# A kernel of attention and a two-layer network: the order of each engine's instructions written out, and other engines for some copies, scalings and relus

## The chip, the cores and the metric

The kernel runs on one core of a Trainium2 chip. A core has five engines with queues of their own: TensorE (PE, matmuls), VectorE (DVE), ScalarE (ACT), GpSimd (POOL) and SyncE (SP, which here only issues transfers). Each engine does its instructions in the order in which the program lists them; an instruction that waits holds up everything behind it on its engine. The time is that of one execution on the device in microseconds (us), and the median of several runs is given.

## The reference

Two parts stand one behind the other; all is float32.

```
scores = q @ k^T / 8                        # B=4, H=8, S=576, D=64; causal mask
a      = softmax(scores)
local  = a @ v
q_p    = where(q > 0, q, exp(q) - 1) + 1
mem    = (q_p @ M_prev) / (q_p . z_prev + 1e-6)
g      = 1 / (1 + exp(-beta))               # one per head
x      = g * mem + (1 - g) * local          # -> 2304 tokens x 512
r      = max(x @ w_in, 0)                   # 512 x 2048
out    = (s * r*r + b) @ w_out              # 2048 x 512
```

## The kernel before

**Attention.** The 32 heads are handled as 16 pairs (`attention(g)`, g = 0 to 15; four pairs make a batch). A pair goes through these steps. PE makes the scores (L383) in three visits, each over some of five row tiles `i`; DVE adds the mask and takes the row minimum of the negated scores (L390, `red`); ACT takes the exponential and its row sum (L396, `ex`); DVE makes the reciprocal of the sums (L435, L436); DVE or POOL scales the probabilities (L402, `scale`, by the table `SCAL`). Beside it `phi(g)` makes q_p from q: a relu (L319, L321 or L323 on ACT, DVE or POOL by `RELU`), an exponential on ACT (L324), a combination on DVE (L325), a product with z (L329, by `ZMUL`), a row sum on DVE (L331) and two products with its reciprocal (L342, by `PUTS`), which go into gaps of the probabilities' tile P. So one transposed tile holds both kinds of weights. PE transposes P in four banks (L463), 58 transposes for a pair; ACT or DVE copies each bank in two halves out of PSUM (L472 to L479, `copy`, by `COPY`); then PE makes the pair's output product (L514) from them, with M_prev and v in the tile V. ACT and DVE split the result into two parts of float32r (L535 and L536, tiles xs and x4).

**Network, first layer.** x @ w_in is made from those split parts, with three matmuls for one product (L580 to L582). 41 of these products, each in two halves of six matmuls, are placed among the attention (`first`), where PE has nothing else; ACT's relu (L603) and a transfer of SP to the DRAM tile r_d follow. They need the split results of the four pairs of a batch, and w_in, which is converted in 20 pieces by ACT, DVE and POOL (`convert`, L560 to L573; `HIGH` and `LOW` say on which engine its two parts are made). The rest of the first layer and the second layer follow behind the attention.

**What sets the order.** All steps of the attention are recorded in a `Plan` (`add`), each with its engine, a duration, a rank, what it reads and writes, and the PSUM tiles it takes (pool S: two tiles of 1024 columns, pool T: four of 512). `deal` then plays them through: at each point each engine takes, among the steps that could start, the one with the lowest rank, and for PE some rules on the changes between its three modes (`full`, `row`, `col`) come first. What it picks is the order in which the instructions are issued. Where PE would be idle in that play, `waits` puts in matmuls whose result is not used (L272, "filling" matmuls). The stages behind the attention are written in another way, by `later` and `tick`, and the change does not touch them.

Of the kernel before, what the change touches and what calls it, by code (L numbers as in the profile page):

```python
# [43 lines left out]
class Plan:  # L44
# [8 lines left out]
    TURN = 110  # L53
    HOLD, WORK, WAIT = (2.5, 3), (1, 5), (0.05, 0.05)
# [23 lines left out]
    def deal(self):  # L78
        ready = {}
# [4 lines left out]

        def put(s):
            s["at"] = max([0.0] + [
                d["end"] + (0.0 if d["eng"] == s["eng"] == "PE" else self.LAT + s["slack"]) for d in s["deps"]])
            ready.setdefault(s["eng"], []).append(s)

        for s in self.steps:  # L90
            if not s["need"]:
                put(s)
        while any(ready.values()):
            best = None
            for eng, some in ready.items():
                t0 = clock.get(eng, 0.0)
                able = []
                for s in some:
                    t = max(t0, s["at"], port if s["port"] else 0.0)
                    for place, pool in s["take"]:  # L100
                        if place is not None:
                            free = sorted(x for x in self.free[pool] if x is not None)
                            n = sum(1 for q in s["take"] if q[1] == pool)
                            t = max(t, free[n - 1] + s["slack"]) if len(free) >= n else None
                            break
                    if t is not None:
                        able.append((t, s))
                if not able:
                    continue
                first = min(t for t, _ in able)  # L110
                now = [(t, s) for t, s in able if t <= first + 0.02]
                if eng == "PE":
                    late = t0 >= self.TURN
                    wait = 0.15 if mode == "full" else self.WAIT[late]
                    same = [(t, s) for t, s in able if s["mode"] == mode and t <= max(t0 + wait, first + 0.02)]
                    rest = [(t, s) for t, s in now if s["mode"] != "full"]
                    if mode == "full" and rest and (
                            max(first - s["at"] for _, s in rest) >= self.HOLD[late] or sum(s["cost"] for _, s in rest) >= self.WORK[late]):
                        now = rest
                    elif same:  # L120
                        now = same
                    elif rest:
                        now = rest
                t, s = min(now, key=lambda x: (x[1]["rank"], x[1]["n"]))
                if best is None or t < best[0]:
# [46 lines left out]
def attention_moe_kernel(  # L172
# [469 lines left out]
    for g in range(NPAIR):  # L642
# [6 lines left out]
        if g % NP == NP - 1:  # L649
# [303 lines left out]
```

## Time and profile before

| | us |
|---|---|
| runs shown: median (lowest to highest, 3 runs) | 552.17 (550.9 to 552.63) |
| profiled execution: first to last instruction (its span) | 549.2 |
| PE busy | 537.4 (98%) |
| ACT busy | 397.7 (72%) |
| DVE busy | 396.5 (72%) |
| POOL busy | 259.6 (47%) |

The span is from the first to the last instruction of the profiled execution; the page gives no other time of that execution. The median of the runs is 3.0 us above the span. Busy time of PE holds the filling matmuls and matmuls that wait while they are in the pipeline, so it isn't a measure of work. A line number is the line of the instruction in the kernel before. In the views below an instruction reads as line, operation, the tile that it writes, `<-`, the tiles that it reads.

### The profile page before, as it was taken

To read this page: it belongs to the slowest core of one execution; us is meant where nothing else is said; L and a number is where in the kernel's file an instruction comes from. 1 tells how busy PE (TensorE), PEld (TensorE's weight loads), DVE (VectorE), ACT (ScalarE), POOL (GpSimd) and SP (SyncE) were. 2 spreads that over 40 slices of the span, in tenths; PEclk is the share of its full clock that TensorE was granted. 3 is DMA by queue.
4 is the path that set the end of the run, shared out by engine and by line. 5 is a ranking of instruction groups with operands and counts; after the bars stand their busy time and mean duration, and the time that the engine had idled before them with its cause. 6 is when DMAs were issued, how large, how long until landed. Compare 5 with 4: busy or idle time off the path is not lost.

```text
span 549.2 us, 11418 instructions
## 1 busy us (share of the span) xinstructions
PE 537.4 (98%) x4078; PEld 443.5 (81%) x4078; DVE 396.5 (72%) x979; ACT 397.7 (72%) x875; POOL 259.6 (47%) x273
## 2 busy tenths in 40 slices
PE   8998999999999999999999999999999999999997
PEld 6666777777777777777778888889999999999996
DVE  5999999999896643234239897434797897888772
ACT  6987898867678945466346577859987987887840
POOL 5882464441445751433100000507669668768760
PEclk9999899999999999999999999999999999999999
DMA  5556676754445333321166655448335344353101
GB/s 187 193 154 187 223 232 174 233 151 156 126 111 175 113 123 106 109 83 57 59 249 258 234 209 187 148 142 291 106 111 167 107 143 137 110 173 103 39 30 38
DMA packets 56665, 81.50 MB, mean 148 GB/s; under 512 B 7584, under 2 KB 39072, under 8 KB 56608
## 3 DMA queue, kind: packets, MB, share of 16 engines
q1 hardware_dynamic: 54064, 78.63, 44.3%
q10 hardware_dynamic: 2544, 2.14, 1.2%
q8 instruction: 32, 0.52, 0.4%
q14 instruction: 25, 0.20, 0.1%
HBM read 57.15 MB, written 23.59 MB: 147 GB/s over the span
## 4 chain that ended last, share of the span: by engine, by line
PE 85%; DVE 8%; ACT 2%; POOL 1%; DMA 1%; issue 1%; DVEq 0%; ACTq 0%; POOLq 0%
PE yps L808 12%; PE yps L812 11%; PE sb L514 7%; PE sb L383 6%; PE hps L580 5%; PE hps L581 5%; PE hps L582 5%; PE yps L811 5%; PE yps L810 5%; PE tb L463 4%; PE tb L580 4%; PE tb L581 3%; PE tb L582 3%; DVE P L390 3%; PE sb L580 3%; PE sb L581 2%
## 5 line engine op out<-in xcount | busy, mean ns | idle before, releaser
L402 POOL TENSOR_SCALAR P<-P,sr,omg 128x192 f32<-128x192 f32 (+4 forms) x118 | 75.9, 657 | 66.2 <-DVE sr L436 41.4
L396 ACT ACTIVATE P<-P,mn 128x448 f32<-128x448 f32 (+4 forms) x160 | 88.5, 559 | 22.0 <-DVE mn L390 20.8
L812 PE MATMUL yps<-rb,op 128*128 128x256 f32 x360 | 101.1, 281 | 0.0
L390 DVE CUSTOM_DVE_ANT_0 P<-sb,mask 128x448 f32<-128x448 f32 (+4 forms) x160 | 71.1, 483 | 17.7 <-PE sb L383 17.6
L808 PE MATMUL yps<-rb,op 128*128 128x512 f32 x216 | 76.9, 397 | 0.0
L812 PEld LDWEIGHTS yps<-rb,op 128*128 128x128 f32 x360 | 67.9, 189 | 0.0
L383 PE MATMUL sb<-qk 64*128 64x288 f32 (+4 forms) x384 | 57.8, 411 | 1.7 <-DMA qk<-in_qk_t_dram 0.9
L788 POOL TENSOR_TENSOR sum<-src 128x512 f32<-128x512 f32 x10 | 12.9, 1294 | 90.6 <-ACT src L772 75.9
L796 POOL TENSOR_TENSOR op<-src,op 128x512 fp32r<-128x512 f32 x30 | 44.0, 1490 | 20.1 <-ACT op L795 20.1
L819 DVE TENSOR_TENSOR yu<-yu,yps 128x256 f32<-128x256 f32 x90 | 36.5, 414 | 21.5 <-PE yps L812 20.4
L383 PEld LDWEIGHTS sb<-qk 64*128 64x128 f32 x384 | 35.6, 187 | 16.2 <-issue 6.1
L463 PEld LDWEIGHTS tb<-ident,P 64*128 64x128 f32 x928 | 37.3, 141 | 13.6 <-issue 3.5
L808 PEld LDWEIGHTS yps<-rb,op 128*128 128x128 f32 x216 | 40.6, 188 | 9.0
L463 PE MATMUL tb<-ident,P 64*128 64x64 f32 x928 | 42.3, 228 | 4.4 <-DVE P L402 2.4
L810 PE MATMUL yps<-rb,op 128*128 128x256 f32 x144 | 40.5, 281 | 0.0
L811 PE MATMUL yps<-rb,op 128*128 128x256 f32 x144 | 40.5, 281 | 0.0
L795 ACT CAST op<-src 128x512 fp32r<-128x512 f32 x50 | 30.4, 614 | 11.9 <-PE yps L812 7.5
L796 DVE TENSOR_TENSOR op<-sum,op 128x512 fp32r<-128x512 f32 x36 | 37.7, 1048 | 0.3 <-ACT op L795 0.2
L472 ACT COPY pt<-tb 128x512 f32<-128x512 f32 x54 | 29.0, 586 | 12.2 <-PE tb L463 7.8
L587 ACT ACTIVATE r<-hps 128x256 f32<-128x256 f32 x62 | 21.8, 384 | 18.5 <-DMA r_d<-r 14.5
L796 POOL TENSOR_TENSOR op<-w1H,op 128x512 fp32r<-128x512 f32 x24 | 34.9, 1482 | 0.0
L396 ACT ACTIVATION_READ_ACCUMULATOR P<-P,mn 128x1 f32 x160 | 31.0, 194 | 0.0
(171 smaller groups left out, 1548.2 us busy)
## 6 DMA issues: line engine op xcount, KB each, us to landing
r_d<-r SPq DMA_DIRECT2D x41, 256.0 KB, 2.4
src<-r_d SPq DMA_DIRECT2D x20, 512.0 KB, 4.8
qk<-in_qk_t_dram SPq DMA_DIRECT2D x15, 576.0 KB, 4.2
raw<-in_moe_w_out_dram SPq DMA_DIRECT2D x16, 512.0 KB, 5.8
w1H<-r_d SPq DMA_DIRECT2D x16, 512.0 KB, 4.4
xa<-in_moe_w_in_dram SPq DMA_DIRECT2D x12, 512.0 KB, 4.5
r_d<-r SPq DMA_DIRECT2D x48, 128.0 KB, 2.0
qs<-in_q_rows_dram SPq DMA_DIRECT2D x16, 320.0 KB, 3.8
```

The source lines that it names most:

```text
L383: nc.tensor.matmul(at(ps, j, o, n), lhsT=qk[rs, 128 * i:128 * i + 128], rhs=qk[rs, S + 64 + c0:S + 64 + c0 + n], start=True, stop=True, ti ...
L390: nc.vector.tensor_tensor_reduce(P[:, j, PB[i] + 64:PB[i] + 64 + n], at(ps, j, o, n), m, -SCALE, 3.0e38, ALU.add, ALU.min, mn[:, j, i:i + 1])
L396: nc.scalar.activation(pt, pt, AF.Exp, scale=-1.0, bias=mn[:, j, i:i + 1], accum_out=sm[:, j, i, 0:1])
L402: e.tensor_scalar(pt, pt, sr[:, j, i:i + 1], omg[:, h:h + 1], ALU.mult, ALU.mult)
L463: nc.tensor.transpose(TB[ps[h]][:, o[h]:o[h] + 64], P[rs, j, c:c + 128], ident[rs, rs], tile_position=(64 * h, 0))
L580: nc.tensor.matmul(ps, lhsT=wH[:, p, fs], rhs=xs[:, 0], start=p == 0, stop=False)
L581: nc.tensor.matmul(ps, lhsT=wH[:, p, fs], rhs=xs[:, 1], start=False, stop=False)
L796: (nc.gpsimd if m in ONPOOL else nc.vector).tensor_sub(L, x, H.bitcast(F32))
L808: nc.tensor.matmul(tile, lhsT=H, rhs=B, start=f == 0, stop=False)
L810: nc.tensor.matmul(ps, lhsT=H, rhs=B[:, 0], start=f == 0, stop=False)
L811: nc.tensor.matmul(ps, lhsT=H, rhs=B[:, 1], start=False, stop=False)
L812: nc.tensor.matmul(ps, lhsT=L, rhs=B[:, 0], start=False, stop=f == KF - 1)
```

## The change

`deal` takes a list `ORDER` with one number for each of the 1402 steps of the attention: on each engine the steps are issued by rising number, and nothing is picked any more. The rules for picking and their constants go. A step's start is still worked out in the play, for the order between the engines and for the filling matmuls, with durations that are partly new. The tables `RELU`, `ZMUL`, `PUTS`, `COPY`, `SCAL`, `HIGH`, `LOW` and `HOME` (the PSUM pool of an FFN product) have new letters: A is ACT, D is DVE, P is POOL. Of the 160 scalings 56 are on DVE, before 42; of the 32 products of phi with its norm 16, before 6; of the 16 products with z 3, before 6. The work on PE is the same, except that 26 filling matmuls are issued, before 35.

```diff
-    def deal(self):
-        ready = {}
+    def deal(self, order):
+        rows = {}
+        for s in sorted(self.steps, key=lambda s: order[s["n"]]):
+            rows.setdefault(s["eng"], []).append(s)
+        for row in rows.values():
+            row.reverse()
...
+            for eng, row in rows.items():
+                if not row or row[-1]["need"]:
                     continue
...
+                s = row[-1]
+                t = max([clock.get(eng, 0.0), port if s["port"] else 0.0] + [
+                    d["end"] + (0.0 if d["eng"] == eng == "PE" else self.LAT) for d in s["deps"]])
...
-    RELU = "AAPAADPAADAAAAAA"
-    ZMUL = "PPPDDDDDDPPPPPPP"
-    PUTS = "PPPDPPPPDDPPPPPP"
-    COPY = ["ADAD", "DAAD", "AAAD", "AAAA", "AAAA", "AAAA", "AAAA", "AAAD", "DDAD", "DAAD", ] + ["AAAD"] * 6
-    SCAL = ["PPPPP", "PPPPP", "DPPPP", "DDDDD", "DPPPP", "PPPDD", "PPPDD", "DDDDD", "PPPDD", "PPDDD", ] + ["PPPPP"] * 6
-    HIGH, LOW = "AAPAPAAAPPAAPPAAPAPA", "DPPDDPDPDDPDDDDDDPDP"
+    RELU = "AAAAAAAADAAADDDP"
+    ZMUL = "PDPDDPPPPPPPPPPP"
+    PUTS = "DDPDPPDDPPPPDDPD"
+    COPY = ["AAAD", "AAAA", "AAAA", "AAAA", "AAAA", "AAAA", "DAAA", "AADD", "AADA", "AAAA", "AAAA", "AADD", "DADA", "DADA", "ADAA", "DDDD"]
+    SCAL = ["PPPPP", "PDPPP", "DPPPP", "PPPPP", "PPPPP", "PDDPD", "PPDPD", "PPPPD", "DDDPP", "DDDPP", "PPPDP", "DDPPD", "PPPDP", "PDPPD", "PDPDP", "DDDDD"]
+    HIGH, LOW = "PPPAAAPAPAAAAAAAAAAA", "PDPDDPPPDDPDDDPPPDDP"
...
-    SCD = (0.11, 0.18, 0.26, 0.34, 0.42)
+    SCD = (0.22, 0.29, 0.36, 0.42, 0.49)
...
-    HOME = "TTTTTTTTTSTTTTTTTTTTTSTSSSTTSSSTSTTSSSTSS"
+    HOME = "TTTTTTTTTTSTTTSTTTTTTTSSSTTTTTSTTTTTSTSSS"
...
+    ORDER = [
+        0, 3, 5, 363, 13, 15, 21, 32, 1, 4, 7, 2, 6, 8, 30, 33, 36, 40, 50, 59, 80, 87, 84, 12, 19, 25, 16, 18, 17, 22, 23, 28, 39, 55, 61, 86, 70, 57, 20,
...
-        for step in plan.deal():
+        for step in plan.deal(ORDER):
```

The rows below are the instructions as the built program lists them on an engine; the line numbers of the changed kernel are lower by 30 in this part (L402 is L372 there). First DVE, before, with the last scalings of pair 3 (P_124 is the tile P of pairs 1, 3, 5, P_123 that of pairs 0, 2, 4; xs are split results of pair 2):

```order
L536 TENSOR_TENSOR xs<-tb_99,xs 128x256
L571 TENSOR_TENSOR w0L<-w_106,w0H 128x256
L564 SCALAR_TENSOR_TENSOR w_107<-xa_105,w_107 128x256
L402 TENSOR_SCALAR P_124<-P_124,sr_122,omg 128x192
L402 TENSOR_SCALAR P_124<-P_124,sr_122,omg 128x320 x2
L390 ISA P_123,mn_117<-sb_97,mask 128x448
L390 ISA mn_117 128x1
L402 TENSOR_SCALAR P_124<-P_124,sr_122,omg 128x64 x2
L402 TENSOR_SCALAR P_124<-P_124,sr_122,omg 128x576 x2
```

DVE in the changed kernel, from the last reciprocal of pair 3 to the last instruction that its output product needs:

```order
L406 RECIPROCAL sr_122<-sr_122 128x2
L312 TENSOR_TENSOR P_124<-qs_114,nrm_116 128x3x2x64
L360 ISA P_123,mn_117<-sb_97,mask 128x576
L360 ISA mn_117 128x1
L506 TENSOR_TENSOR x_141<-tb_100,x_141 128x64
L506 TENSOR_TENSOR xs<-tb_100,xs 128x256
L506 TENSOR_TENSOR xs<-tb_99,xs 128x256
L531 TENSOR_SCALAR w_106<-w_106 128x256
L360 ISA P_123,mn_117<-sb_96,mask 128x576
L360 ISA mn_117 128x1
L532 SCALAR_TENSOR_TENSOR w_106<-xa_103,w_106 128x256
L312 TENSOR_TENSOR P_124<-qs_114,nrm_116 128x2x2x64
```

The scalings of pair 3 are no longer on DVE; reductions of the next pair stand there, and the products of phi with its norm come last.

PE before, from the last score visit ahead of pair 3's output product (L514) on:

```order
L383 MATMUL sb_96<-qk_109 128x288
L514 MATMUL tb_99<-F_128,V_126 64x320 x2
L514 MATMUL tb_99<-pt,V_126 64x256 x2
L514 MATMUL tb_99<-F_128,V_126 64x128 x2
L514 MATMUL tb_101<-F_128,V_126 64x256 x2
L514 MATMUL tb_101<-pt,V_126 64x256 x6
L514 MATMUL tb_101<-F_128,V_126 64x128 x2
L383 MATMUL sb_97<-qk_110 128x448 x2
L383 MATMUL sb_97<-qk_110 128x64 x2
L383 MATMUL sb_96<-qk_110 128x320 x2
L383 MATMUL sb_96<-qk_110 128x192 x2
L580 MATMUL tb_98<-xs,w0H 128x512
```

PE in the changed kernel at the same product (L484 there):

```order
L353 MATMUL sb_96<-qk_110 128x320 x2
L353 MATMUL sb_96<-qk_110 128x192 x2
L484 MATMUL tb_98<-F_128,V_126 64x320 x2
L484 MATMUL tb_98<-pt,V_126 64x256 x2
L484 MATMUL tb_98<-F_128,V_126 64x128 x2
L484 MATMUL tb_99<-F_128,V_126 64x256 x2
L484 MATMUL tb_99<-pt,V_126 64x256 x6
L484 MATMUL tb_99<-F_128,V_126 64x128 x2
L550 MATMUL tb_100<-xs,w0H 128x512
```

The first two score visits of pair 5 (`qk_110`) are now ahead of the product, the second of them right before it, and the first layer's matmuls begin right behind it.

ACT before, at the copies of pair 1's transposes (L472 to L479; tiles F and pt are the copies):

```order
L472 COPY pt<-tb_98 128x8x64
L472 COPY pt<-tb_100 128x8x64
L324 ACTIVATE qs_113<-qs_113 128x640
L396 ACTIVATE P_123,sm_119<-P_123,mn_117 128x576
L474 COPY F_128<-tb_98 128x2x4x64
L474 COPY F_128<-tb_100 128x2x4x64
L396 ACTIVATE P_123,sm_119<-P_123,mn_117 128x576
```

ACT in the changed kernel at the same copies (L442 to L449 there):

```order
L442 COPY pt<-tb_98 128x8x64
L442 COPY pt<-tb_99 128x8x64
L366 ACTIVATE P_123,sm_119<-P_123,mn_117 128x576
L444 COPY F_128<-tb_100 128x2x4x64
L442 COPY pt<-tb_99 128x8x64
L444 COPY F_128<-tb_98 128x2x4x64
L442 COPY pt<-tb_101 128x8x64
L449 COPY F_128<-tb_100 128x2x2x64
L446 COPY F_128<-tb_99 128x2x3x64
```

All four banks of the pair, eight copies, are now on ACT; before, two of the banks were on DVE.

## Rows read from the trace of the kernel before

Columns of the windows: stretch and length in us, then busy us and instruction count of each engine, the granted clock of PE as a share of full speed, the share of the DMA engines, GB/s.

**Rows 1.** Windows of the four stages; each engine's busy us, instructions, clock.

```profile
core 0: us, PE busy (x) PEld busy (x) DVE busy (x) ACT busy (x) POOL busy (x), PEclk, DMA share, GB/s
0.00:60.80 60.80, 53.14 (x524) 38.52 (x524) 53.50 (x204) 49.22 (x146) 35.03 (x56) 0.97 0.57 177
60.80:281.30 220.50, 219.92 (x1865) 164.84 (x1863) 144.05 (x459) 153.34 (x407) 94.23 (x128) 1.00 0.44 138
281.30:367.50 86.20, 86.20 (x471) 75.06 (x470) 61.67 (x119) 58.90 (x129) 8.46 (x6) 1.00 0.60 211
367.50:549.20 181.70, 178.17 (x1224) 165.08 (x1223) 137.23 (x199) 136.28 (x194) 121.92 (x84) 1.00 0.38 121
```

**Rows 2.** Waits of PE from 64 to 281 us, longest: total, times, longest.

```profile
PE sb L514 <- DVE mn L390: 0.3, 1, 0.3
```

**Rows 3.** PE's timeline, 44 to 67 us: start, us, line, tiles, count.

```profile
44.98 0.50 PE L580 MATMUL tb<-xs,w0H 128*128 128x512 f32 x1 [0.63 <-ACT pt L472]
...
46.56 0.76 PE L514 MATMUL tb<-F,V 128*64 128x320 f32 x4
...
49.85 2.05 PE L272 MATMUL tb<-ident 128*128 128x128 f32 x16
...
53.34 0.28 PE L463 MATMUL tb<-ident,P 64*128 64x64 f32 x2 [0.65 <-DVE P L402]
55.33 0.79 PE L463 MATMUL tb<-ident,P 64*128 64x64 f32 x10 [1.72 <-DVE P L402]
...
60.84 0.76 PE L514 MATMUL tb<-F,V 128*64 128x320 f32 x4
...
64.12 2.11 PE L383 MATMUL sb<-qk 64*128 64x448 f32 x16
66.16 0.50 PE L580 MATMUL tb<-xs,w0H 128*128 128x512 f32 x1
```

**Rows 4.** DVE's timeline around the last scalings of pair 3.

```profile
52.92 1.50 DVE L402 TENSOR_SCALAR P<-P,sr,omg 128x192 f32<-128x192 f32 x3
...
54.88 1.50 DVE L402 TENSOR_SCALAR P<-P,sr,omg 128x64 f32<-128x64 f32 x4
```

**Rows 5.** Scalings (L402) from 46 to 56.4 us: DVE, then POOL.

```profile
46.00:56.40 10.40, 4.32 (x10) 0.00 (x0) 0.95 0.56 163
```

**Rows 6.** Groups of one shape: count, busy us, mean ns, idle before.

```profile
L472 ACT COPY pt<-tb 128x512 f32<-128x512 f32 x54 | 29.0, 586 | 12.2 <-PE tb L463 7.8 <-PE sb L514 4.4
...
L390 DVE CUSTOM_DVE_ANT_0 P<-sb,mask 128x576 f32<-128x576 f32 x32 | 23.0, 751 | 8.0 <-PE sb L383 7.9
...
L472 DVE COPY pt<-tb 128x512 f32<-128x512 f32 x10 | 6.4, 667 | 0.0
...
L479 DVE COPY F<-tb 128x256 f32<-128x256 f32 x12 | 5.0, 418 | 13.6 <-PE tb L463 13.5
```

**Rows 7.** Waits of ACT from 0 to 61.3 us.

```profile
ACT pt L472 <- PE tb L463: 2.7, 3, 1.6
ACT w L560 <- DVE w0L L571: 2.1, 1, 2.1
ACT P L396 <- DVE mn L390: 1.7, 3, 1.1
ACT L635 <- PEq L936: 1.6, 1, 1.6
ACT gin L638 <- DMA gin<-in_beta_dram: 1.4, 1, 1.4
...
ACT qs L324 <- POOL phr L323: 0.7, 1, 0.7
```

**Rows 8.** Window of ACT between the last copies of pairs 3 and 4.

```profile
61.20:82.40 21.20, 19.82 (x56) 1.00 0.76 246
```

**Rows 9.** Scalings on DVE: ns least, median, most.

```profile
L402 DVE TENSOR_SCALAR P<-P,sr,omg x42: 302/509/1395, 38.9 to 157.1; 128x448 f32<-128x448 f32 x12, 128x576 f32<-128x576 f32 x12, 128x64 f32<-128x64 f32 x8, 128x320 f32<-128x320 f32 x6
```

**Rows 10.** Window of PE at the lower clock.

```profile
55.40:58.80 3.40, 3.40 (x32) 0.51 0.36 142
```

More of the change, by code (lines that the diff above doesn't have):

```diff
@@ L83, in deal @@
         done = []
[L85 to L93, printed above, removed]
-            best = None
[L95 to L108, printed above, removed]
-                    continue
[L110 to L125, printed above, removed]
@@ new lines, in deal @@
+        while any(rows.values()):
+            best = None
+            for eng, row in rows.items():
+                if not row or row[-1]["need"]:
+                    continue
+                s = row[-1]
+                t = max([clock.get(eng, 0.0), port if s["port"] else 0.0] + [
+                    d["end"] + (0.0 if d["eng"] == eng == "PE" else self.LAT) for d in s["deps"]])
+                for _, pool in s["take"][:1]:
+                    free = sorted(x for x in self.free[pool] if x is not None)
+                    t = max(t, free[len(s["take"]) - 1]) if len(free) >= len(s["take"]) else None
+                if t is not None and (best is None or t < best[0]):
@@ L128, in deal @@
             t, s = best
-            ready[s["eng"]].remove(s)
+            rows[s["eng"]].pop()
             s["start"] = t
@@ L318, in phi @@
         if RELU[g] == "A":
-            add("ACT", 0.72, lambda: nc.scalar.activation(PHR, q, AF.Relu), r0 + RPS[g], [("q", u)], ["phr"])
+            add("ACT", 0.64, lambda: nc.scalar.activation(PHR, q, AF.Relu), r0 + RPS[g], [("q", u)], ["phr"])
         elif RELU[g] == "D":
-            add("DVE", 0.45, lambda: nc.vector.tensor_scalar(PHR, q, 0.0, None, ALU.max), r0 + RPS[g], [("q", u)], ["phr"], port=True)
+            add("DVE", 0.40, lambda: nc.vector.tensor_scalar(PHR, q, 0.0, None, ALU.max), r0 + RPS[g], [("q", u)], ["phr"], port=True)
         else:
-            add("POOL", 0.88, lambda: nc.gpsimd.tensor_scalar(PHR, q, 0.0, None, ALU.max), r0 + RPS[g], [("q", u)], ["phr"])
-        add("ACT", 0.72, lambda: nc.scalar.activation(q, q, AF.Exp), r0 + RPS[g] + 0.01, [], [("q", u)])
+            add("POOL", 1.80, lambda: nc.gpsimd.tensor_scalar(PHR, q, 0.0, None, ALU.max), r0 + RPS[g], [("q", u)], ["phr"])
+        add("ACT", 0.64, lambda: nc.scalar.activation(q, q, AF.Exp), r0 + RPS[g] + 0.01, [], [("q", u)])
         add("DVE", 0.73, lambda: nc.vector.scalar_tensor_tensor(q, q, 1.0, PHR, ALU.min, ALU.add), r0 + RPS[g] + 0.1,
@@ L328, in phi @@
         ez, mul = side(ZMUL[g])
-        add(ez, 1.54 if ez == "POOL" else 0.83, lambda: mul.tensor_mul(
+        add(ez, 1.54 if ez == "POOL" else 0.74, lambda: mul.tensor_mul(
             PHR, q, z.unsqueeze(1).to_broadcast([128, 5, 2, D])), r0 + RQS[g] + 0.01, [("q", u), ("z", u)], ["phr"], port=True)
@@ L435, in attention @@
             add("DVE", 0.08, lambda s=s, t=t: nc.vector.tensor_reduce(t, s, AX.X, ALU.add), r + RSR, keys, inv)
-            add("DVE", 0.12, lambda t=t: nc.vector.reciprocal(t, t), r + RSR, [], inv)
+            add("DVE", 0.09, lambda t=t: nc.vector.reciprocal(t, t), r + RSR, [], inv)
             for k, i in enumerate(mine):
@@ L494, in attention @@
             for h in range(2):
-                cost = dict(A=0.48 if k < 3 else 0.30 + 0.13 * h, D=0.58 if k < 3 else 0.33 + 0.13 * h)
+                cost = dict(A=0.48 if k < 3 else 0.26 + 0.11 * h, D=0.58 if k < 3 else 0.33 + 0.13 * h)
                 c = COPY[g][k]
@@ L566, in convert @@
         if HIGH[n] == "P":
-            add("POOL", 0.6, lambda: nc.gpsimd.tensor_scalar(H, w, 1.0, 1.0, ALU.mult, ALU.mult), rank, [B_], [("WH", n)])
+            add("POOL", 0.8, lambda: nc.gpsimd.tensor_scalar(H, w, 1.0, 1.0, ALU.mult, ALU.mult), rank, [B_], [("WH", n)])
         else:
@@ L602, in first @@
         add("PE", cost, lambda: mm1(part(), b, f, 1), 999, x(1) + w(1), [("h", m), "seq"], mode="full")
-        add("ACT", 0.58, lambda: nc.scalar.activation(r, part(), AF.Relu), -1, [("h", m)], [("r", m % 3)], give=[(ps, 0, pool)])
+        add("ACT", 0.49, lambda: nc.scalar.activation(r, part(), AF.Relu), -1, [("h", m)], [("r", m % 3)], give=[(ps, 0, pool)])
         add("SP", 0.4, lambda: nc.sync.dma_start(r_d[b][:, f], r), -1, [("r", m % 3)], ["st"], bytes=262144)
```

11 lines of the change are left out of this document (4 added, 7 removed), and 48 rows, old and new, of the table ORDER.

## The prediction

> **What bounds the kernel now.** I read the windows of the stages first, then the waits of PE, PE's timeline where its waits lie, and last the engines that it waited for. The table of stages [rows 1] shows PE at 219.92 of 220.50 us between 60.8 and 281.3 us, 86.20 of 86.20 in the stage behind it and 178.17 of 181.70 in the last; only the first 60.8 us have a real hole, with 53.14. The longest wait of PE from 64 us to the end of the attention is 0.3 us [rows 2]. From 60.8 us on the time is therefore the sum of PE's work, since the first layer's matmuls (FFN) fill every gap, and nothing that DVE, ACT or POOL save there comes out at the end. Before it the FFN can't fill, since its input is the output of pairs 0 to 3.
>
> So the time hangs on one moment: the start of the output product of pair 3 (L514), now 60.84 us [rows 3]; call it X. The product of pair 2 starts at 46.56 and its successor, a run of filling matmuls, at 49.85 [rows 3]. In the 11 us from there to X PE has only pair 3's transposes and one visit of scores, yet it waits twice for `DVE P L402`, 0.65 and 1.72 us, and fills between. L402 is the scaling of the probabilities. From 46 to 56.4 us all ten scalings of pair 3 run on DVE, 4.32 us, while POOL does none [rows 5]; the last four end at 54.88 + 1.50 = 56.38 [rows 4]. DVE is full there (53.50 of 60.8 busy, most of the rest being the start [rows 1]); ACT has 49.22 and POOL 35.03.
>
> **The change part by part.** PE's matmuls are the same but for nine fillers fewer; the code behind the attention keeps its order on every engine, so the last two stages cost nothing and give nothing. The edits to durations alone emit nothing once the order is written out.
>
> *DVE up to X.* Ahead of the last DVE instruction that X needs, DVE now does 137 steps, before 139. Gone are the ten scalings of pair 3 (4.32 us [rows 5]) and eight copies out of PSUM, four at 0.667 and four of about 0.418 [rows 6], 4.3 us. Come are seven score reductions, four products of phi with its norm, one product with z, two scalings of pair 1 and two weight steps: sixteen, which I put at 0.42 us each, an estimate half way between the least and the median scaling [rows 9], 6.7 us (bounds 16 x 0.30 = 4.8 and, all as long as the widest reduction at 0.751 [rows 6], 12.0). The last one would end at 56.4 - 8.6 + 6.7 = 54.5. Behind it come ten transposes (0.79 [rows 3]) and two copies (under 0.586 each [rows 6]): X no earlier than about 56.2 by DVE.
>
> *ACT up to X.* The copies and one relu go here: 105 steps instead of 100, and the longer kinds; eight copies more (four at 0.586 [rows 6], four shorter; about 3.2 back to back) and a relu, less casts, weight steps and exponentials. I count +2.3 us (bounds: five at 0.2 and five at 0.586 more, 1.0 to 2.9). ACT waited 1.6 + 1.4 at the start, which stays, and 2.7 for transposes, 2.1 for a weight step of DVE, 1.7 for reductions and 0.7 for POOL's relu of pair 2 [rows 7]. That relu is now ACT's own, so its wait goes; the 2.7 and 2.1 hang on DVE's and POOL's queues, which get shorter ahead of them. If none of these waits goes, X is 60.84 + 2.3 = 63.1. If 5.5 of them go (2.7, 2.1, 0.7), it is 57.6. I take 58.0: nearly all of it, since DVE alone would allow 56.2 and ACT is what ends last. That is -2.8 us.
>
> *PE around X.* The order puts both first score visits of pair 5 ahead of X; now they stand behind it, from 64.12 to 66.16, 2.04 us [rows 3]. The first half FFN product, now ahead of X from 44.98 to 46.56, 1.58 us, goes behind it and joins a run there, where it loses its switch of mode (I take 1.4). There is also one run of FFN fewer among the attention (30, before 31), some 0.2 us by the same difference. What PE has to do behind X shrinks by 2.0 - 1.4 + 0.2 = 0.8; I take 0.9 with the other small switches.
>
> *Behind X.* ACT has 44 steps between the last copies of pairs 3 and 4, before 39, about 2.8 us more (five at 0.586 [rows 6]), and was busy 19.82 of 21.20 us there [rows 8]. PE has three FFN halves more in that stretch and two score visits fewer, 3 x 1.4 - 2.0 = 2.2 us, and 1.4 us of ACT's idle time are there too; so nothing should be left over. That is an average over a queue in strict order, and I add 0.4 us; bounds 0 and 2.8.
>
> Sum: -2.8 - 0.9 + 0.4 = -3.3 us. The profiled span is 549.2 us, so 545.9 for it; the runs shown have a median of 552.17, 3.0 above the span, and the difference goes over: 548.9.
>
> One rule speaks against the moves between DVE and POOL. A DVE scaling took 0.302 at least and 0.509 in the middle, but one took 1.395 [rows 9]; the ten that now go to POOL ran while POOL had no scaling [rows 5]. The Trainium skill, page "SBUF — State Buffer", section "Who interferes with whom", says that a DVE instruction in a two-port mode or with two SBUF inputs and a GpSimd instruction that reads SBUF hold a shared port pair for their whole length, and the other blocks. By that rule the ten come back to DVE as blocking, and the sum would be -0.4 instead of -3.3 (worked out under the rivals). The row with 1.395 agrees that such stretching happens; no row here shows it for all ten.
>
> **Rivals.**
>
> *More than forecast.* ACT keeps only the start's waits and DVE's 56.2 decides; the later stalls shrink also. For it: POOL has 35.03 of 60.8 us and takes the ten scalings with room [rows 1]. Against it: one queue on ACT in strict order with 2.3 us more. X = 56.2: -4.6 - 0.9 - 0.5 = -6.0, 546.2.
>
> *No difference.* ACT loses the relu's wait and some of the transposes', no more: X = 61.0, +0.2 - 0.9 + 0.4 = -0.3, 551.9. For it: ACT's wait for DVE's weight step [rows 7] comes from a buffer that is still shared.
>
> *The port.* POOL's ten scalings stretch DVE by as much as they had taken on it, 4.3 us, and two thirds of it lies ahead of the last needed instruction: DVE's 56.2 becomes 59.1, and its reductions hold ACT as long, so X = 58.0 + 2.9 = 60.9 and the time 551.8, within the same band. This is the result that the rule of the Trainium skill, page "SBUF — State Buffer", would give.
>
> *Slower.* ACT's queue is the price: it waits as long as before and has 2.3 us more ahead of X (63.1), and the later stretch up to pair 4 lacks 1.0: +2.3 - 0.9 + 1.0 = +2.4, 554.6. It decides once X is past 63.0. For it: ACT is the fullest engine behind X [rows 8]. Against it: the waits had releasers that the change moves earlier.
>
> *The clock*, a risk and no case of its own. PE ran at a granted 0.51 from 55.4 to 58.8 [rows 10], the lower of its levels (1.2 instead of 2.4 GHz), after the waits of the rows above. With nine fillers fewer it may fall at another place; if it falls on an output product (3.28 us from 60.84 to 64.12 [rows 3]) it costs up to 1.7 us. The Trainium skill, page "TensorE: Matmul & The Clock Gate", section "Why this matters for your kernels", warns of gaps between bursts for this reason; the trace agrees, since the drop follows the waits. I keep this inside the ranges.
>
> **How the numbers follow.** Two times of this kernel differ measurably from about 0.3% on, 1.65 us. Forecast, 548.9 with 547.0 to 550.5 as its own range: 0.47. More: 0.20. No difference: 0.16. The port: 0.06. Slower: 0.11. Faster by over 0.3% is the forecast and the first rival, 0.67; same, with the port, 0.22; slower 0.11. The range goes from 545.2 (X at 56.2 with every later stall gone) to 552.8, which leaves out most of the slower case and a little below.
>
> **What would show it.** In the profile after: the product of pair 3 starts between 56.5 and 59.7 us, and the attention ends as much earlier, less or more a microsecond; the stages behind it keep 86.2 and 181.7 us; the wait of PE for `DVE P` of the scalings is gone, and what PE waits for ahead of X is a copy of ACT. ACT's waits up to X fall from the 10.2 us of the six rows [rows 7] to between 4 and 6. Wrong if X stays over 60, if PE waits over 2 us between X and the end of the attention, or if DVE's stretch of scalings comes back as longer instructions of DVE beside POOL's.

## The result, and the profile after

The changed kernel takes 542.99 us (median of four runs, 542.56 to 543.25), the kernel before, beside it on the same chip, 551.53 (550.81 to 552.63). The ratio is 0.9846, interval 0.9831 to 0.9862: 8.5 us faster, where 3.3 were forecast, and outside the forecast range. The profiled span is 541.0 us. Lines of the attention stand 30 lower than before: L514 is now L484, L402 is L372, L390 is L360.

The stages of the changed kernel, in the columns of [rows 1]:

```profile
0.00:54.90 54.90, 47.46 (x516) 34.70 (x516) 48.69 (x195) 50.59 (x151) 38.09 (x60) 1.00 0.62 195
54.90:273.10 218.20, 218.11 (x1853) 164.02 (x1853) 156.86 (x485) 150.87 (x406) 88.74 (x102) 1.00 0.44 140
273.10:359.30 86.20, 86.20 (x471) 75.05 (x470) 61.61 (x119) 58.66 (x129) 8.48 (x6) 1.00 0.60 211
359.30:541.00 181.70, 178.17 (x1224) 165.08 (x1223) 138.93 (x199) 136.21 (x194) 121.77 (x84) 1.00 0.38 121
```

The last two stages are as long as before, 86.2 and 181.7 us. The first ends 5.9 us earlier, and the stretch behind it is 2.3 us shorter, 218.20 instead of 220.50. PE's timeline has the product of pair 2 at 43.76 (46.56 before) and that of pair 3, X, at 54.95 (60.84 [rows 3]); the two score visits that ran behind X now end ahead of it (the second is shown):

```profile
43.76 0.76 PE L484 MATMUL tb<-F,V 128*64 128x320 f32 x4 [0.64 <-ACT pt L442]
...
53.77 1.08 PE L353 MATMUL sb<-qk 64*128 64x320 f32 x7
54.95 0.76 PE L484 MATMUL tb<-F,V 128*64 128x320 f32 x4
```

What PE waits for up to 55 us (total, times, longest) is no scaling of DVE any more. The 2.4 us of `DVE P L402` in [rows 3] are gone, and 0.6 for POOL's scalings stand in their place:

```profile
PE sb L353 <- DVE mn L360: 2.2, 4, 0.8
PE tb L484 <- ACT pt L442: 1.3, 2, 0.7
...
PE tb L433 <- POOL P L372: 0.6, 2, 0.3
```

This is all that ACT waits for from 5.9 to 58.5 us. Before, it has five waits of 0.7 to 2.7 us there, 7.9 together: four of [rows 7], and 0.7 for a scaling of POOL that [rows 7] do not show:

```profile
ACT P L366 <- DVE mn L360: 1.1, 1, 1.1
```

That one belongs to the start and ends at 5.98 us, where ACT's first exponential begins; before, 1.1 of the 7.9 are this wait. The window from 6 to 54.9 us, in the columns of [rows 1]:

```profile
6.00:54.90 48.90, 43.00 (x494) 30.80 (x492) 47.98 (x190) 48.87 (x148) 36.00 (x48) 1.00 0.62 200
```

ACT is busy 48.87 of 48.90 us, and DVE, the fuller of the two before [rows 1], still 47.98. The last thing X needs is ACT's:

```profile
54.09 0.54 ACT L446 COPY F<-tb 128x384 f32<-128x384 f32 x1
54.46 0.44 ACT L449 COPY F<-tb 128x256 f32<-128x256 f32 x1
```

The ten scalings of pair 3 run on POOL from 43.81 and end at 53.18 us, where DVE's ended at 56.38 [rows 4]:

```profile
43.81 4.54 POOL L372 TENSOR_SCALAR P<-P,sr,omg 128x192 f32<-128x192 f32 x7 [2.17 <-ACT pt L442]
49.33 1.78 POOL L372 TENSOR_SCALAR P<-P,sr,omg 128x576 f32<-128x576 f32 x2 [0.98 <-DVE sr L406]
...
52.11 1.07 POOL L372 TENSOR_SCALAR P<-P,sr,omg 128x64 f32<-128x64 f32 x1
```

One thing in DVE and POOL was not in the prediction. The DVE instruction of phi (two inputs out of SBUF) of pairs 0 to 2 was long in the kernel before; POOL's rows of the same stretches lie over it:

```profile
11.49 1.34 DVE L325 SCALAR_TENSOR_TENSOR qs<-qs,phr 128x640 f32<-128x640 f32 x1
21.60 1.08 DVE L325 SCALAR_TENSOR_TENSOR qs<-qs,phr 128x640 f32<-128x640 f32 x1
32.29 1.33 DVE L325 SCALAR_TENSOR_TENSOR qs<-qs,phr 128x640 f32<-128x640 f32 x1
43.99 0.77 DVE L325 SCALAR_TENSOR_TENSOR qs<-qs,phr 128x640 f32<-128x640 f32 x1
```

```profile
8.55 4.86 POOL L402 TENSOR_SCALAR P<-P,sr,omg 128x64 f32<-128x64 f32 x8 [5.78 <-ACT P L396]
...
20.12 3.52 POOL L402 TENSOR_SCALAR P<-P,sr,omg 128x448 f32<-128x448 f32 x5 [0.39 <-ACT P L396]
...
31.36 1.59 POOL L402 TENSOR_SCALAR P<-P,sr,omg 128x448 f32<-128x448 f32 x2
```

Each of the three takes what is left of the scaling that POOL is in when it starts (0.66, 0.41 and 0.67 us), and 0.66 to 0.68 us more. The fourth, at 43.99, started while POOL stood still, and took 0.77. In the kernel after, the four of pairs 0 to 3 take 0.81 to 0.83 us; they stand in POOL's gaps, or begin as POOL ends:

```profile
26.31 0.81 DVE L295 SCALAR_TENSOR_TENSOR qs<-qs,phr 128x640 f32<-128x640 f32 x1
```

```profile
20.16 5.62 POOL L372 TENSOR_SCALAR P<-P,sr,omg 128x64 f32<-128x64 f32 x8 [1.06 <-DVE w L531]
27.20 1.66 POOL L299 TENSOR_TENSOR phr<-qs,z 128x640 f32<-128x640 f32 x1 [1.43 <-DVE qs L295]
```

That is 1.3 us less on DVE (1.34 + 1.08 + 1.33 less 3 x 0.82). It comes mostly from the written order: with before's order on after's engines (old_order_new_engines below) the first two still take 1.34 and 1.16 us, the third 0.82; with after's order on before's engines (order_old_engines) they take 0.82, 1.02 and 0.81. The planner's rule on a shared `port` is in both kernels and is not what is new.

### The profile page after: what moved, and what is told of

Same layout as the page of the kernel before. It is cut to its first block, busy times and chain, and to the rows that moved or that the text cites. A ratio compares the mean times of both kernels' runs of the same rounds, so it can differ in the third digit from the quotient of the medians.

```text
span 541.0 us, 11347 instructions
## 1 busy us (share of the span) xinstructions
PE 529.9 (98%) x4060; PEld 438.9 (81%) x4060; DVE 406.1 (75%) x997; ACT 396.3 (73%) x879; POOL 257.1 (48%) x251
## 4 chain that ended last, share of the span: by engine, by line
PE 91%; DVE 4%; ACT 2%; DMA 1%; issue 1%; SPq 0%; POOL 0%; DVEq 0%; ACTq 0%
PE yps L829 12%; PE yps L833 11%; PE sb L484 7%; PE sb L353 7%; PE tb L550 6%; PE hps L550 5%; PE hps L551 5%; PE hps L552 5%; PE tb L551 5%; PE tb L552 5%; PE tb L433 5%; PE yps L832 5%; PE yps L831 5%; PE sb L550 2%; DVE P L360 2%; PE sb L552 2%
## 5 line engine op out<-in xcount | busy, mean ns | idle before, releaser
L366 ACT ACTIVATE P<-P,mn 128x320 f32<-128x320 f32 (+4 forms) x160 | 90.0, 570 | 22.7 <-DVE mn L360 22.7
L372 POOL TENSOR_SCALAR P<-P,sr,omg 128x64 f32<-128x64 f32 (+4 forms) x104 | 74.8, 731 | 60.3 <-DVE sr L406 43.7
L360 DVE CUSTOM_DVE_ANT_0 P<-sb,mask 128x64 f32<-128x64 f32 (+4 forms) x160 | 72.4, 483 | 22.9 <-PE sb L353 21.9
L353 PE MATMUL sb<-qk 64*128 64x288 f32 (+4 forms) x384 | 56.1, 410 | 2.7 <-DVE mn L360 2.2
L353 PEld LDWEIGHTS sb<-qk 64*128 64x128 f32 x384 | 34.1, 187 | 17.3 <-issue 8.5
L433 PEld LDWEIGHTS tb<-ident,P 64*128 64x128 f32 x928 | 36.1, 139 | 9.7 <-issue 4.8
L433 PE MATMUL tb<-ident,P 64*128 64x64 f32 x928 | 39.6, 225 | 1.8 <-POOL P L372 0.6
L817 DVE TENSOR_TENSOR op<-sum,op 128x512 fp32r<-128x512 f32 x36 | 38.9, 1079 | 0.3 <-ACT op L816 0.2
L299 POOL TENSOR_TENSOR phr<-qs,z 128x640 f32<-128x640 f32 x13 | 21.8, 1680 | 24.7 <-DVE qs L295 13.5
L366 ACT ACTIVATION_READ_ACCUMULATOR P<-P,mn 128x1 f32 x160 | 32.8, 205 | 0.0
```

What stands on the lines that cost most here:

```text
L353: nc.tensor.matmul(at(ps, j, o, n), lhsT=qk[rs, 128 * i:128 * i + 128], rhs=qk[rs, S + 64 + c0:S + 64 + c0 + n], start=True, stop=True, ti ...
L360: nc.vector.tensor_tensor_reduce(P[:, j, PB[i] + 64:PB[i] + 64 + n], at(ps, j, o, n), m, -SCALE, 3.0e38, ALU.add, ALU.min, mn[:, j, i:i + 1])
L366: nc.scalar.activation(pt, pt, AF.Exp, scale=-1.0, bias=mn[:, j, i:i + 1], accum_out=sm[:, j, i, 0:1])
L372: e.tensor_scalar(pt, pt, sr[:, j, i:i + 1], omg[:, h:h + 1], ALU.mult, ALU.mult)
L433: nc.tensor.transpose(TB[ps[h]][:, o[h]:o[h] + 64], P[rs, j, c:c + 128], ident[rs, rs], tile_position=(64 * h, 0))
L817: (nc.gpsimd if m in ONPOOL else nc.vector).tensor_sub(L, x, H.bitcast(F32))
```

## The experiments

The first theory was ORDER and ACT: the written order took ACT's waits away, so X is ACT's start plus its work. It lost. LOOP took its place: under the written order ACT and DVE wait for one another by turns with next to no slack on either, so no one engine's sum sets X. Of LOOP the runs bear out that work added to either engine delays X and that work taken from one alone gives next to nothing; its claim for both at once they do not. That ACT and DVE are each full behind the start (48.87 and 47.98 of 48.90 us) would give the same two results, and no run tells it from waiting by turns. Shown without any theory is that neither half of the change is worth anything without the other.

Here is every run. X and the stretch from X to the end of the last output product are from one profiled execution each; the total is a median; the ratio is to the kernel before, run beside it. The common foot is control_old.

```
                          X     behind X   total   ratio to before (95%)
before                  60.84    220.49   551.53
after                   54.95    218.18   542.99   0.985 (0.983 to 0.986)
common foot             61.54    220.95   553.00   1.003 (1.002 to 1.004)
  + after's order       67.03    232.83   571.39   1.036 (1.034 to 1.038)
  + after's engines     61.22    226.05   556.99   1.010 (1.009 to 1.012)
  + pair 3's scalings   60.61    220.54   551.17   1.000 (0.999 to 1.000)
before, new durations   62.82    233.43   569.10   1.032 (1.031 to 1.034)
after, scalings back    58.80    218.30   547.26   0.992 (0.991 to 0.994)
after, copies back      58.77    218.24   546.70   0.992 (0.991 to 0.994)
after, relus to POOL    57.73    218.23   545.90   0.991 (0.989 to 0.992)
after, ACT more         59.01    218.23   545.39   0.990 (0.988 to 0.991)
after, DVE more         56.82    218.16   546.09   0.990 (0.988 to 0.992)
after, ACT less         54.76    218.25   542.70   0.985 (0.983 to 0.986)
after, DVE less         54.75    218.16   543.10   0.986 (0.984 to 0.987)
after, both less        53.85    218.21   542.82   0.985 (0.983 to 0.987)
after, visits behind X  55.01    225.52   550.20   0.998 (0.997 to 1.000)
after, no fillers       56.42    218.20   545.79   0.990 (0.988 to 0.992)
```

Executions of one kernel lie further apart where something was changed in after (dve_plus 544.65 to 546.82, no_fill 544.3 to 547.46), so X of one profile and the median need not agree to a microsecond. Ten kernels have the same stretch behind X within 0.14 us, so such differences presumably lie ahead of X. act_plus was profiled in its longest execution (546.92), and dve_plus, dve_minus, both_minus and no_fill in their shortest (544.65, 542.59, 541.73 and 544.30): there the median counts for more than X.

### Order and engines apart

**control_old**, the foot of the next three: after's code with before's numbers of the order, tables of engines and places.

```
-    RELU = "AAAAAAAADAAADDDP"            # likewise ZMUL, PUTS, COPY, SCAL, HIGH, LOW, HOME, ORDER
+    RELU = "AAPAADPAADAAAAAA"
```

> After's code with before's order, engines and places of tiles, so before but for a few filling matmuls that the new durations plan: the common foot of the runs on order and engines. Expected: as before within 0.3%, 549.8 to 553; the product of pair 3 at 60 to 61.5 us. If it lies over 554 or under 548, the fillers or the new durations act by themselves, and the runs on order and engines have to be read against it.

It is 1.5 us over before, at the upper edge of what was expected, and for a reason of its own: DVE, ACT and POOL have the same instructions in the same order as in before, but the new durations plan PE's fillers elsewhere. (The trace has two records for each filling matmul; runs are counted in records here.) Before had two runs of four ahead of X, at 56.05 and 58.24; here the last four stand at 53.49, and the clock that the chip granted PE in the window up to X is half (0.70 in before over 56.0 to 60.8):

```profile
56.00:61.50 5.50, 4.93 (x40) 3.63 (x40) 5.30 (x22) 5.45 (x17) 1.22 (x2) 0.50 0.50 165
```

The first four matmuls of X took 1.24 us here, 0.76 in [rows 3]; X is 0.7 us later and its product 0.5 us longer.

**order_old_engines**: after with before's seven tables (the first line of the diff above, without HOME and ORDER).

> After's written order on every engine, with before's tables of engines (relus, scalings, copies, weight steps). Here a written row that names an engine is followed on that engine, so before's choice of engines puts DVE at 49.0 us and ACT at 47.5 us of work up to the product of pair 3 (sums of durations of both traces; after itself 44.4 and 50.7, before 45.6 and 48.4). Theory ORDER (it is the order that removed ACT's waits, whoever does a step): ACT still waits for little behind its start, DVE is the fullest and the product of pair 3 starts at 57 to 59.5 us, total 545.5 to 548. Rival ENGINES (the relief of DVE is what removed the waits): ACT's waits of 5 us and more are back, the product starts at 60 us or later, total 549 to 553.

ORDER fails. What ENGINES named came, X behind 60 and ACT's waits back, but far past its range: X 67.03, total 571.4. ACT's longest waits from 7 us to there, of 12.8 us in all:

```profile
ACT qs L294 <- POOL phr L293: 4.0, 1, 4.0
ACT w L530 <- DVE w0L L541: 3.6, 2, 2.5
ACT w0H L539 <- DVE w L534: 2.2, 3, 1.7
ACT pt L442 <- PE tb L433: 1.3, 2, 1.1
```

**old_order_new_engines**: the other half (HOME and ORDER of before, the tables of after).

> Before's own order, step by step, and after's tables of engines. DVE has 37.6 us and ACT 51.6 us of work up to the product of pair 3. Theory ORDER: DVE is relieved by 8 us and yet ACT keeps most of its 7 us of waits, since they come from what stands ahead of what in the queues; the product of pair 3 starts at 58.5 us or later, total 547.5 to 552. Rival ENGINES: the waits go with DVE's relief, ACT ends its 51.6 us 0.9 us later than after does, the product starts at 56 us, total 543.5 to 545.5.

X is 61.22, as ORDER said, though by the sums of durations in the expectations DVE has 8 us less to do than in before (37.6, 45.6); the total passes its upper end, since the stretch behind X grew by 5.6 us too. Together with the run before it: order alone +18.4 us on the foot, engines alone +4.0, both -10.0. The gain can't be split into shares; the order belongs to these engines.

**old_scal3**, the prediction's own term alone, on the foot:

```
-    SCAL = ["PPPPP", "PPPPP", "DPPPP", "DDDDD", ...
+    SCAL = ["PPPPP", "PPPPP", "DPPPP", "PPPPP", ...
```

> The common foot (after's code with before's order, engines and places: product of pair 3 at 61.54 us, 553.0) with one edit: the ten scalings of pair 3 on POOL instead of DVE, 4.5 us less on DVE. Theory FOR-EACH-OTHER (an engine's relief is worth something only in an order that uses it): under before's order POOL comes to these scalings late or PE waits for the next in line, so the product starts at 60 us or later and the total stays over 551. Rival RELIEF (the prediction's step: DVE's scalings are what ended last there, the two waits of PE for them, 2.4 us, go): the product at 58 to 59.5 us, total 549.5 to 551.

X 60.61, total 551.17: FOR-EACH-OTHER, by the narrow margin that its bound left. It gains 1.8 us on the foot, whose clock had fallen, and nothing on before. PE's two waits for DVE went, and POOL comes later than DVE did:

```profile
51.73 0.40 POOL L537 TENSOR_SCALAR w0H<-w 128x256 fp32r<-128x256 f32 x1 [2.93 <-DVE w L534]
52.12 2.19 POOL L372 TENSOR_SCALAR P<-P,sr,omg 128x192 f32<-128x192 f32 x3
...
54.98 2.77 POOL L372 TENSOR_SCALAR P<-P,sr,omg 128x64 f32<-128x64 f32 x4
```

In the old order the scalings stand on POOL behind a weight step that waits 2.93 us for DVE, and four of them take 2.77 us, where DVE took 1.50: they end at 57.75, DVE's ended at 56.38 [rows 4].

**durations_alone**: before, with only the new numbers of durations (`add("ACT", 0.72` to `0.64`, and so on).

> Before, with the new durations of the change alone: before's rules order the steps again by them, on before's engines; no written order. Theory FOR-EACH-OTHER: durations move a few steps, ACT keeps 4 us or more of waits behind its start, total 549 to 556. Rival DURATIONS (truer durations are enough for the rules to find what the written order has): the product before 58 us, total below 548.

X is 62.82, 2 us behind before's, with 233.4 us behind it; 569.1 is 13 us above the upper end. ACT waits 5.5 us for DVE's reductions from 0 to 66 us, 1.3 of them at the start:

```profile
ACT P L396 <- DVE mn L390: 5.5, 5, 2.1
```

So before's rules don't find the order by the new durations; they lose by them.

### One edit undone under the new order

**scal3_dve**: `SCAL[3]` "PPPPP" to "DDDDD". **copy_old**: the first three of `COPY` "AAAD", "AAAA", "AAAA" to "ADAD", "DAAD", "AAAD". **relu_pool**: `RELU` "AAAA..." to "AAPP...".

> After, with the ten scalings of pair 3 on DVE again instead of POOL, and nothing else: some 4 us of work more on DVE ahead of the product of pair 3. Theory LOOP (under the written order ACT and DVE wait for one another by turns with next to no slack on either, so work added to either delays the product by about as much as it lasts, as twice the row sum on DVE did, +1.9 us for 2.2): the product starts at 58 to 59.5 us, total 545.5 to 547.5. Rival SMALL (pair 3's scalings hid beside ACT's copies, and the other edits brought the gain): the product below 55.9 us, total below 544.0.

> After, with four copies of pairs 0 to 2 on DVE again, where before had them (two of a 128x512 tile, two of F): DVE has about 2.2 us more, ACT about 1.8 us less, up to the product of pair 3. Theory LOOP: DVE's addition counts and ACT's relief gives little of it back, since the order still makes DVE's reductions wait behind the copies: the product at 55.5 to 57.5 us, total 543.6 to 545.6. Rival ACT (the fullest queue alone sets the product): the product 1 to 1.8 us earlier, total 541.2 to 542.2.

> After, with the relu of pairs 2 and 3 on POOL instead of ACT: ACT has 2 x 0.74 = 1.5 us less up to the product of pair 3, POOL 2 x 1.81 = 3.6 us more of which it has 17 us idle there. Theory LOOP: ACT's relief is worth something only where it is not waited for through POOL at once; the exponential of the same tile waits for the longer relu, so between -0.8 and +0.8 us, total 542.2 to 543.8. Rival ACT: the product 1.3 us earlier, total 541.4 to 541.9. Rival POOL (the relu stands in the chain with its full length, as the wait of 0.7 us in before for pair 2): +1.0 to +2.2.

X is later by 3.85, 3.82 and 2.78 us: LOOP for the scalings; for the copies its direction, X 1.3 us past its end; for the relus its rival POOL, 0.6 over its end. The expectation of copy_old counts half of the edit: a letter of `COPY` is a bank, a bank is two copies, and so eight copies go to DVE and not four, 4.3 us by the means of [rows 6] (4 x 0.667 and 4 x 0.418). Against that, 3.82 is what LOOP says of work added to DVE. Two of the three take work from the full engine, ACT (two relus, eight copies), and yet it ends later, since it now waits. The waits of ACT from 7 us to X, in the three kernels in this order:

```profile
ACT pt L442 <- PE tb L433: 2.7, 2, 2.4
ACT w L530 <- DVE w0L L541: 0.6, 1, 0.6
```

```profile
ACT P L366 <- DVE mn L360: 3.0, 2, 2.6
ACT phr L289 <- DVE nrm L301: 1.1, 1, 1.1
ACT w L530 <- POOL w0L L543: 1.0, 2, 0.8
```

```profile
ACT qs L294 <- POOL phr L293: 3.0, 2, 1.6
```

The three add up to 10.5 us of X, where the whole change is 5.9: such undoings are no shares of the gain.

### Work added and work taken away

**act_plus** and **dve_plus**, for pairs 1 to 3:

```
+            n_relu = 2 if g in (1, 2, 3) else 1
+    ... lambda: [nc.scalar.activation(PHR, q, AF.Relu) for _ in range(n_relu)]
+        n_sum = 2 if g in (1, 2, 3) else 1
+    ... lambda: [nc.vector.tensor_reduce(n, PHR, AX.X, ALU.add) for _ in range(n_sum)]
```

> After, with the relu of pairs 1 to 3 issued twice on ACT (the same values into the same tile): 3 x 0.64 = 1.9 us of work more on ACT ahead of the product of pair 3, and none on another engine. Theory ACT (ACT is full from 6 us to the last copy, so its sum of work sets the product of pair 3): the product starts at 56.9 us, total 544.5 to 545.5 (+1.6 to +2.3). Rival CHAIN (the chain over DVE, PE and POOL sets it, and that ACT is full beside it is a coincidence): under +0.7, total below 543.8.

> After, with the row sum of pairs 1 to 3 issued twice on DVE (the same values into the same tile): 3 x 0.73 = 2.2 us of work more on DVE ahead of the product of pair 3. Theory ACT: DVE's last instruction that the product needs ended at 52.74 us, 2.2 us ahead of the product; a part of the 2.2 us is lost in DVE's own waits, the rest delays transposes and ACT by little: total +0.2 to +1.2. Rival DVE (DVE with its 44.4 us and the chain behind it sets the product): the product 2.2 us later, total +1.8 to +2.6, 544.8 to 545.6.

The totals rise by 2.4 and 3.1 us. ACT's extra three relus come to some 2.3 us by these rows (one pair of three), and the total, 545.39, is what theory ACT said:

```profile
25.16 1.53 ACT L290 ACTIVATE phr<-qs 128x640 f32<-128x640 f32 x2
```

X is 4.06 us later in that profile, the longest execution of the four, where DVE's reductions wait 2.9 us for scores (0.8 in after) and ACT 2.3 for the reductions. DVE's extra 2.5 us put X back by 1.87 in the shortest execution, and the median total by 3.1: theory ACT said 0.2 to 1.2 and is wrong there.

**act_minus**, **dve_minus** and **both_minus**, which leave out most of some relus, of some row sums, and of both:

```
+            few = slice(0, 1) if g in (1, 2, 3) else slice(None)
+    ... nc.scalar.activation(PHR[:, few, few, few], q[:, few, few, few], AF.Relu)
+        less = slice(0, 1) if g in (2, 3) else slice(None)
+    ... nc.vector.tensor_reduce(n[:, less], PHR[:, less], AX.X, ALU.add)
```

> After, with the relu of pairs 1 to 3 cut on ACT to one column of 640 (the rest of the tile is left as it was, so phi of these pairs is not computed rightly): about 3 x 0.6 = 1.8 us less on ACT up to the product of pair 3, nothing added anywhere. Theory ACT (the full queue of ACT sets the product): the product 1.5 to 1.9 us earlier, total 541.0 to 541.6. Theory LOOP (ACT and DVE have no slack against each other, so relief of one alone stops at the other's queue): the product less than 0.9 us earlier, total 542.0 to 543.2. Rival RIGID (the order was found for exactly these durations, and any change of them, also a shorter step, throws waits up): later, total over 543.8.

> After, with the row sum of pairs 2 and 3 on DVE cut to one of five columns of heads (the norms of the others are those of an earlier pair, so these outputs are not right): about 2 x 0.55 = 1.1 us less on DVE up to the product of pair 3. Theory ACT: nothing, the product within 0.3 us of 54.95, total 542.5 to 543.4. Theory LOOP: the product 0.2 to 0.7 us earlier, total 542.2 to 543.0. Rival RIGID: total over 543.8.

> After, with both cuts of the two kernels before this one together (relu of pairs 1 to 3 on one column, row sum of pairs 2 and 3 on one of five): 1.8 us less on ACT and 1.1 us less on DVE. Theory LOOP: the product 1.2 to 2.2 us earlier, more than both cuts alone add up to, total 540.6 to 541.8. Theory ACT: as the cut on ACT alone, within 0.3 us. Rival RIGID: total over 543.8.

1.6 us less on ACT (three relus of 0.19 to 0.24 us for 0.72 to 0.79) moves X by 0.19; 1.1 us less on DVE by 0.20; both together by 1.10. The medians move by -0.3, +0.1 and -0.2. So ACT's sum alone does not set X, and ACT's theory has fallen by act_minus and dve_plus: an engine that never stops can still be in step with another. RIGID has fallen too. LOOP holds for the cut on ACT; dve_minus lies 0.1 over its total and fits theory ACT as well. That both cuts together give more than the two alone add up to is not shown: X is 0.1 short of LOOP's lower end in the shortest of four executions (541.73, the others 542.14 to 543.99), and the median, 542.82, is 1.0 over its upper end. What holds X when both engines are relieved stays open.

### The visits, and the fillers

**s5_behind**: the numbers of the two first score visits of pair 5 in ORDER, moved on PE alone behind X.

```
-  ... two score visits of pair 5, then the output product of pair 3
+  ... the output product of pair 3, then the two visits
```

> After, with the two first score visits of pair 5 moved behind the product of pair 3 on PE, as before had them; DVE, ACT and POOL keep their order. Theory FILL (ahead of that product PE has room, behind it every microsecond of PE counts): the product starts where it does in after, 54.95 us, or up to 0.5 us earlier, and the stretch behind it grows by the 2.04 us that the visits take, total 544.5 to 545.2. Rival NONE (the moves of PE's work across the product are worth nothing, the stretch behind it got shorter by its stalls alone): total 542.6 to 543.5.

X stays, 55.01, as FILL said; the stretch behind grew by 7.3 us and not by 2.0. DVE's order has the visits' reduction next, and everything behind it waits:

```profile
61.55 0.62 DVE L360 CUSTOM_DVE_ANT_0 P<-sb,mask 128x448 f32<-128x448 f32 x1 [8.79 <-PE sb L353]
```

ACT's weight step waits in turn for DVE's, and PE fills 2.6 us:

```profile
65.44 0.41 ACT L539 CAST w0H<-w 128x256 fp32r<-128x256 f32 x1 [4.47 <-DVE w L534]
```

```profile
63.74 2.62 PE L242 MATMUL tb<-ident 128*128 128x128 f32 x22
```

The product of pair 3 also ran at a granted 0.62 (window 55.0 to 60.2) and took 5.26 us, 3.36 in after. So the price of 2.04 us for the visits holds only where the other queues move along; here they did not, and the run doesn't tell what the visits alone are worth.

**no_fill**: `if n > 1 and free` to `if n > 99 and free` in the planner's `waits`.

> After without the filling matmuls that the plan puts into PE's gaps in the attention; the ones at the start stay. Theory ORDER (DVE, ACT and POOL set the product of pair 3, fillers only occupy PE): the product within 0.5 us of 54.95, total 542.4 to 543.6. Rival CLOCK (the fillers hold the clock up there; without them the granted clock falls to half in a stretch ahead of the product or on it, as in the common foot, where 0.50 from 56 to 62 us cost 1.7 us): the product or its length +1 to +3 us, total 544 to 546.

CLOCK: X 1.47 us later (in the shortest of four executions), total 2.8 up, inside its range. PE's windows show where. Without fillers:

```profile
10.00:16.00 6.00, 2.90 (x21) 1.60 (x19) 5.77 (x31) 6.00 (x17) 4.55 (x7) 1.00 0.88 283
16.00:18.00 2.00, 2.00 (x12) 1.94 (x14) 1.18 (x5) 2.00 (x10) 2.00 (x4) 0.56 0.17 64
```

The kernel after, with 20 records of fillers in that stretch:

```profile
10.00:16.00 6.00, 5.46 (x41) 4.17 (x41) 5.88 (x31) 6.00 (x20) 4.89 (x8) 1.00 0.84 279
16.00:18.00 2.00, 2.00 (x36) 1.95 (x34) 1.94 (x5) 2.00 (x9) 2.00 (x3) 1.00 0.35 95
```

PE had 2.90 us of work in the 6 us, the granted clock falls to 0.56, near its lower level of 1.2 GHz, for the next 2, DVE's reductions wait 1.9 us for scores up to X (0.8 in after), and the delay stays.

## Why the prediction was wrong

What it said right: the time hangs on X; the stages behind keep 86.2 and 181.7; PE's wait for DVE's scalings goes and a copy of ACT stands last ahead of X; PE has no wait listed from 58 us to the end of the attention. The miss of 5.9 us has three parts: X 3.1, the stretch behind it 1.8, and 1.0 for the 3.0 us between span and median, which are 2.0 in the kernel after. The last is no effect of the change: the span of 549.2 lies 1.7 below the shortest of the three runs shown (550.9), and beside the kernel after the median of before was 551.53. The first two err the same way: both gains were put too small.

**ACT up to X** is the step that failed. It took ACT's work as +2.3 us and let 5.1 of its waits go. By the windows ACT is busy 50.59 of 54.90 us, before 49.22 of 60.80 [rows 1]: work +1.4, idle 11.6 down to 4.3, that is 7.3 less. Of the 3.1 us on X, 0.9 are the work and 2.2 the waits. The 2.7, 2.1 and 0.7 us that were weighed all went. So did what was left in place or not listed: the 0.7 for reductions behind the start, the 0.7 for POOL's scaling, and two short waits of 0.5 together. Only the start's 4.3 us stayed. The sign that ACT's waits fall to between 4 and 6 thus came true, but from 11.5 us and not from the 10.2 of six rows.

**DVE up to X** was given as a floor, 56.2, and X went below it. The last DVE instruction that X needs starts at 52.33 and takes 0.41, so it ends at 52.74 instead of 54.5:

```profile
52.33 0.41 DVE L312 TENSOR_TENSOR P<-qs,nrm 128x256 f32<-128x256 f32 x1
```

The floor took DVE's instructions at their lengths and its waits as they were. But "DVE is full there" hid 1.3 us of stretch beside POOL, in rows of 1.08 to 1.34 us that were in the trace, and short waits for scores and exponentials, 2.1 us up to X. By the windows, DVE was busy 49.1 us up to the end of that last instruction (53.50 less 4.4 behind 56.38) and is now 46.5 (48.69 less 2.2): -2.6, of which 1.3 is the stretch. That leaves 1.3 for the balance of steps, which was put at -1.9; 1.0 more came from its waits.

**The port** went the other way: the change moved ten scalings to POOL and DVE got less stretched. The Trainium skill, page "SBUF — State Buffer", section "Who interferes with whom", says that a DVE instruction with two inputs in SBUF contends with a GpSimd instruction that reads SBUF, over a port pair that is locked for one of them. The rows at 11.49, 21.60 and 32.29 us agree with it, each as long as the rest of POOL's scaling and 0.66 to 0.68 us more, and so does the one at 43.99. The prediction weighed it as a price of the engines and did not ask whether the new order keeps such pairs apart. DVE's 576-wide reductions have a mean of 750 ns up to X, 747 before.

**PE around X and behind it**: -0.9 and +0.4 forecast, -2.3 measured. Counted in both traces from each matmul's start to the next one's, the score matmuls of the stretch take 2.4 us less (16 fewer), the FFN matmuls 0.5 more (six more), the transposes 0.5 less, and the output products the same; PE's idle time, 0.58 before and 0.09 now, is in these. Forecast were 2.0 less, 1.2 more (1.4 for the six, 0.2 back for a run) and nothing for transposes. PE changes from one kind of matmul to another 112 times there, before 118; no run shows whether that is the reason. The +0.4 for ACT's strict queue was not needed: behind X the stretch is 218.16 to 218.30 us in ten kernels whose X lies between 53.85 and 59.01, so it is PE's sum there, as the prediction's first paragraph said.

**The edits to durations** were said to emit nothing. They place the fillers, and by control_old that alone is 1.5 us, with the granted clock at 0.50 up to X. The price of the clock on an output product, up to 1.7 us, was low as well: in s5_behind the product took 1.9 us more.

Two figures of the prediction do not follow from its own terms. The lower end of the range, 545.2, is told as X at 56.2 with every later stall gone, which is the first rival's 546.2; and half way between 0.302 and 0.509 is 0.41, not 0.42, which is 0.2 us over sixteen steps.

Of the rivals, More had the mechanism (ACT keeps only the start's waits) and stopped at DVE's floor. The slower case was no fancy: order or engines alone cost 5 to 20 us over before.

## What to carry to other kernels

Where queues in strict order wait for each other, price a rewritten order by two ends, all waits behind the start gone and none gone, and don't let one engine's present waits stand as another's floor: ACT's 49.22 us of [rows 1], the 2.3 added and the waits of its start (1.6, 1.4 and 1.1 in [rows 7]) would have made 55.6 here. X came out at 54.95, since ACT's work grew by 1.4 and not 2.3, and though ACT alone was not what bound it. Test an order and the engines that it was made for together; half of such a change tells nothing of the other half. Before moving one engine's row of an order by hand, look what stands next in the other queues. Set the total of a profiled execution beside the other executions' before you read a microsecond out of it.

## What the runs showed of the hardware

Records of a queue that never drains grow longer, though its work does not. In the kernel after the same relu on ACT reads, over 38 us without a stop:

```profile
7.53 0.72 ACT L289 ACTIVATE phr<-qs 128x640 f32<-128x640 f32 x1
12.84 0.72 ACT L289 ACTIVATE phr<-qs 128x640 f32<-128x640 f32 x1
22.73 0.75 ACT L289 ACTIVATE phr<-qs 128x640 f32<-128x640 f32 x1
34.88 0.79 ACT L289 ACTIVATE phr<-qs 128x640 f32<-128x640 f32 x1
45.24 0.85 ACT L289 ACTIVATE phr<-qs 128x640 f32<-128x640 f32 x1
```

From its start to the start of ACT's next instruction it is 0.63, 0.64, 0.63 and 0.64 us in the last four: the records overlap, and more so as time goes on. With 1.6 us taken off ACT the last one reads 0.77, and in copy_old, where ACT stops ahead of the third, that one is short again:

```profile
23.27 0.74 ACT L289 ACTIVATE phr<-qs 128x640 f32<-128x640 f32 x1 [1.10 <-DVE nrm L301]
37.98 0.72 ACT L289 ACTIVATE phr<-qs 128x640 f32<-128x640 f32 x1
```

So durations read from such a stretch are too high, by up to 0.13 us here, and short waits can hide in the overlap.
